# Linear attention and gated FFN in four layers: the second attention layer's queries of two token groups by seven block products

## The chip, the cores and the metric

The kernel runs on one core of one Trainium2 chip. The metric is the device time of one execution in microseconds (us); a lower time is better. The profiles are of one profiled execution each, with its own time beside its span (from the first to the last instruction).

## The reference

Four residual layers on a sequence of S = 2048 tokens with D = 1024: attention block A, FFN block B, A again, B again, with the same weights both times. Everything is bf16 at the boundary.

```python
def A_ref(x, wqkv, wo):             # H = 32 heads of 32
    q, k, v = split(x @ wqkv)
    phi = lambda t: where(t > 0, t + 1, exp(t)) + 1e-6
    pq, pk = phi(q), phi(k)
    kv = einsum("bhsd,bhse->bhde", pk, v)
    z = einsum("bhsd->bhd", pk)
    num = einsum("bhqd,bhde->bhqe", pq, kv)
    den = einsum("bhqd,bhd->bhq", pq, z)[..., None] + 1e-6
    return merge_heads(num / den) @ wo

def B_ref(x, w_gate, w_up, w_down): # F = 3584
    return ((x @ w_gate) * (x @ w_up)) @ w_down

x = x + A_ref(layernorm(x), wqkv, wo)
x = x + B_ref(layernorm(x), w_gate, w_up, w_down)
x = x + A_ref(layernorm(x), wqkv, wo)
x = x + B_ref(layernorm(x), w_gate, w_up, w_down)
```

## The kernel before

X (all 2048 x 1024 activations) stays in SBUF. Tokens are in 16 tiles of 128, four tiles to a group of 512, so there are four groups. SBUF work space is 17 `slots` of 8 KB a partition and 12 `temps` of 2 KB; PSUM is eight `banks` of 128 x 512 fp32. All three are queues: `get()` takes the one that was put back longest ago, at the time the program is written, so the order of the gets decides which physical bank an operation lands in and for whose last reader it waits. The order of instructions on each engine is the order in which the Python code issues them.

The layers are numbered `li` = 0 (attention), 1 (FFN), 2 (attention), 3 (FFN). `layer_A(li, ahead)` has two phases.

**Keys and values.** In layer 0 `kv_eight` makes them tile by tile with eight matmuls of 512 columns a block. In layer 2 `kv_seven` does it by a seven-product scheme (Strassen-Winograd): the weights and the transposed, normalized tokens are cut into 2 x 2 blocks, sums of blocks are made on VectorE (`w_sum`, `x_sum`), and a unit of 256 tokens of half a group needs seven products for K and seven for V, in the order `SEQ`, in place of eight each. ScalarE copies partial sums out of PSUM and VectorE adds them back. Five banks serve it (`bk`: ak, av, ck, cv, b), three more (`kvp`) gather K'V over all tokens in `kp` (line 533). The last two tiles' `kp` are left to `rest()`.

**Queries and outputs.** A loop over steps `i` runs one instruction sequence by steps of 128 features of a group (8 steps a group, 32 in all):

- `den_step` of step i - 4: one matmul for the denominators (line 801), Ln and Exp of it on ScalarE (803, 807), one multiply on VectorE (810);
- `q_step` of step i: eight matmuls of 512 columns (787), then phi: Exp on ScalarE (311), a minimum with add and a maximum with add on VectorE (312, 314);
- `fold` at steps 4 to 11, in which the K'V blocks are multiplied into `wo`, which was loaded by two DMAs of 1 MB on the SyncE (SP) queue, the first at plan step 90 of `kv_seven`, the second after its last unit;
- `out_step` of step i - 12: eight matmuls (818) and one add into X on VectorE (820).

At step 0 `rest()` and `finish_kv()` end the K'V sums and make the masked blocks `kvm`, `zb`. In layer 0 `scale_begin(1)` and `scale_end(1)` at steps 30 and 33 work out the scale of the down weights: a transpose on TensorE and some ten one-column steps on VectorE.

The last phase of the loop also carries what the next layer needs (`ahead`): LayerNorm of the first eight tiles (`ln_stats` 237 and 240, `ln_norm` 261 to 267, then a DMA transpose in `tr_tile`), the first two weight blocks (`W.load`; in the second FFN these come from a cache in DRAM), and block sums `t_sums`. Tile u has its three parts at steps 20 + 2u, 21 + 2u, 22 + 2u.

The FFN (`ffn_pass`, `quad`, `down_seven`) uses seven products as well: line 950 for gate and up, 1190 for down, both with 512 columns to a matmul. The one exception is the very last output block, two halves of which have 256 columns.

Of the kernel before, what the change touches and what calls it, by code (L numbers as in the profile page):

```python
# [9 lines left out]
ACT = mybir.ActivationFunctionType  # L10
# [25 lines left out]
def kernel(  # L36
# [11 lines left out]
    nc = tc.nc  # L48
# [37 lines left out]
    def v3(s, n):  # L86
        return s[:].rearrange("p (k n) -> p k n", n=n)
# [411 lines left out]
    def kv_seven(kvp):  # L499
        plan = {}  # L500

        def at(step, f, *args):
            plan.setdefault(step, []).append((f, args))
# [223 lines left out]
        return rest  # L727

    def layer_A(li, ahead):
        kvp = [banks.get() for _ in range(3)]  # L730
        rest = kv_eight(li, kvp) if li == 0 else kv_seven(kvp)

        kvx = slots.get()
        kvm, kvT, zb = (v3(kvx, P)[:, r * KD:(r + 1) * KD, :] for r in range(3))

        def finish_kv():
            for b in range(3):
                nb = min(3, KD - 3 * b)
                src = kvp[b][:, 0:nb * VW].rearrange("p (c f) -> p c f", f=VW)
                nc.vector.tensor_copy(out=z[:, 3 * b:3 * b + nb], in_=src[:, :, P])  # L740
                for j in range(nb):
                    if li == 0:
                        nc.vector.tensor_tensor(out=kvm[:, 3 * b + j, :], in0=src[:, j, 0:P], in1=mask[:],
                                                op=ALU.mult)
                    else:
                        nc.vector.scalar_tensor_tensor(out=kvm[:, 3 * b + j, :], in0=src[:, j, 0:P],
                                                       scalar=kaps[:, 2:3], in1=mask[:], op0=ALU.mult, op1=ALU.mult)
            for c in range(KD):
                nc.vector.tensor_scalar(out=zb[:, c, :], in0=mask[:], scalar1=z[:, c:c + 1], scalar2=None,
                                        op0=ALU.mult)  # L750
# [12 lines left out]
        def fold(c):  # L763
            if not M:
                M.extend(slots.get() for _ in range(DC))
            for n in range(DC):
                b = banks.get()
                nc.tensor.matmul(out=b[:], lhsT=kvT[:, c, :], rhs=v3(wA["o"][n], NB)[:, c, :], start=True, stop=True)  # L768
                if n == 0:
                    nc.scalar.copy(out=v3(M[n], NB)[:, c, :], in_=b[:])  # L770
                else:
                    nc.vector.tensor_copy(out=v3(M[n], NB)[:, c, :], in_=b[:])
                banks.put(b)
            if c == KD - 1:
                slots.put(*wA.pop("o"))

        pq = {}
        pqs = {}

        def q_step(g, c):  # L780
            w3 = h3 if li else v3
            xnT = w3(xnTs[(li, g)], NB)
            w = w3(wA["q"][c // (NB // P)], NB)
            j = c % (NB // P)
            b = banks.get()
            for k in range(KD):
                nc.tensor.matmul(out=b[:], lhsT=w[:, k, j * P:(j + 1) * P], rhs=xnT[:, k, :],  # L787
                                 start=(k == 0), stop=(k == KD - 1))
            pq[(g, c)] = temps.get()
            phi(b, pq[(g, c)][:].bitcast(BF16)[:, 0:G], 1 if li else None)  # L790
            banks.put(b)
            if c == KD - 1:
                slots.put(xnTs.pop((li, g)))
                if g == NG - 1:
                    slots.put(*wA.pop("q"))

        def den_step(g, c):
            t = pq.pop((g, c))
            p = t[:].bitcast(BF16)[:, 0:G]
            b = banks.get()  # L800
            nc.tensor.matmul(out=b[:], lhsT=zb[:, c, :], rhs=p, start=True, stop=True)  # L801
            r = temps.get()
            nc.scalar.activation(out=r[:], in_=b[:], func=ACT.Ln, bias=epss[:, 2:3] if li else eps6[:],
                                 scale=1.0)
            banks.put(b)
            rb = r[:].bitcast(BF16)[:, 0:G]
            nc.scalar.activation(out=rb, in_=r[:], func=ACT.Exp, scale=-1.0)
            if c == 0:
                pqs[g] = slots.get()
            nc.vector.tensor_tensor(out=v3(pqs[g], G)[:, c, :], in0=p, in1=rb, op=ALU.mult)  # L810
            temps.put(r, t)

        def out_step(g, j):
            tl, n = divmod(j, DC)
            t = g * TPG + tl
            b = banks.get()
            for c in range(KD):
                nc.tensor.matmul(out=b[:], lhsT=v3(pqs[g], G)[:, c, tl * P:(tl + 1) * P],  # L818
                                 rhs=v3(M[n], NB)[:, c, :], start=(c == 0), stop=(c == KD - 1))
            nc.vector.tensor_tensor(out=X[:, t, n * NB:(n + 1) * NB], in0=X[:, t, n * NB:(n + 1) * NB],  # L820
                                    in1=b[:], op=ALU.add)
# [7 lines left out]
        for i in range(NQ + OLAG):  # L829
            if i >= LAG and i - LAG < NQ:  # L830
                den_step(*divmod(i - LAG, KD))
            if i < NQ:
                q_step(*divmod(i, KD))
# [7 lines left out]
            if i >= OLAG:  # L841
                out_step(*divmod(i - OLAG, KD))
# [449 lines left out]
```

## Time and profile before

| | us |
|---|---|
| median of 3 runs | 1498.21 (1497.66 to 1498.67) |
| the profiled execution | 1497.95 |
| its span | 1496.0 |
| TensorE busy | 1489.4 (100% of the span) |
| VectorE busy | 986.6 (66%) |
| ScalarE busy | 811.0 (54%) |
| GpSimd busy | 89.9 (6%) |
| keys and values of the second attention layer | 758.24 to 865.4 |
| its queries and outputs | 865.4 to 985.05 |

In the profile PE is TensorE's matmuls, PEld its weight loads, DVE VectorE, ACT ScalarE, POOL GpSimd, SP SyncE. Rows of the timeline give start, duration, engine, line, operation, tiles, count; a merged row of several matmuls lasts from the first start to the modelled end of the last. Rows of the groups give count, then busy time and mean duration in ns, then the idle time before with what ended it. Rows of the chain of waits give start, duration and line of each piece of the chain that ended last.

### The profile page before, as it was taken

How to read it: one execution, taken by the hardware profiler on the slowest of the kernel's cores; microseconds unless marked ns; L12 is line 12 of the kernel's file. 1: busy time of each engine (PE TensorE's matmuls, PEld its weight loads, DVE VectorE, ACT ScalarE, POOL GpSimd, SP SyncE). 2: the span in 40 equal slices, each digit the busy share in tenths (PEclk: the TensorE clock that was granted, in tenths of full speed). 3: DMA queues.
4: the chain of work that ended last, by engine and by line, in shares of the span. 5: the costliest groups of instructions: out<-in, count | busy, mean ns of one | idle time of the engine just before them, and what ended most of it. 6: DMA issues, size and time to landing. Idle time of an engine off the chain costs nothing.

```text
span 1496.0 us, 18407 instructions
## 1 busy us (share of the span) xinstructions
PE 1489.4 (100%) x7121; PEld 685.0 (46%) x7121; DVE 986.6 (66%) x1662; ACT 811.0 (54%) x1184; POOL 89.9 (6%) x46
## 2 busy tenths in 40 slices
PE   9999999999999999999999999999999999999999
PEld 4454444444444444444444444444444444444444
DVE  6567989988677666657877686854445844444452
ACT  4678875777558477764557675623335213333420
POOL 0000004963000000000000000000000000000000
DMA  8696146465469788758531101464332788343613
GB/s 246 172 306 232 58 90 198 132 213 157 131 199 309 260 260 260 251 212 249 183 85 26 39 29 45 118 235 166 134 125 97 190 266 320 113 169 113 210 61 130
DMA packets 220087, 253.90 MB, mean 170 GB/s; under 512 B 68576, under 2 KB 196192, under 8 KB 209248
## 3 DMA queue, kind: packets, MB, share of 16 engines
q1 hardware_dynamic: 219712, 252.47, 53.5%
q8 instruction: 55, 0.90, 0.2%
q10 hardware_dynamic: 288, 0.26, 0.1%
q14 instruction: 32, 0.26, 0.1%
HBM read 196.08 MB, written 40.89 MB: 158 GB/s over the span
## 4 chain that ended last, share of the span: by engine, by line
PE 97%; DVE 2%; DMA 1%; ACT 0%; SPq 0%; issue 0%; DVEq 0%; ACTq 0%
PE b L950 45%; PE b L1190 23%; PE b L650 7%; PE b L787 7%; PE b L818 7%; PE b L579 6%; PE b L801 1%; DMA s<-in_A_wqkv_dram 1%; PE b L669 1%; PE b L768 0%; PE b L533 0%; DVE st L237 0%; ACT f L295 0%; DVE X L1163 0%; DVE X L820 0%; DVE s L301 0%
## 5 line engine op out<-in xcount | busy, mean ns | idle before, releaser
L950 PE MATMUL b<-s,s 128*128 128x512 f16 x3136 | 677.7, 379 | 0.0
L950 PEld LDWEIGHTS <-s 128*128 128x128 f16 x3136 | 306.8, 98 | 369.8
L1190 PE MATMUL b<-s,s 128*128 128x512 f16 (+1 forms) x1582 | 339.1, 377 | 0.0
L966 DVE TENSOR_TENSOR f<-f,b 128x512 f32<-128x512 f32 x232 | 159.1, 686 | 223.9 <-ACT f L955 209.7
L955 ACT COPY f<-b 128x512 f32<-128x512 f32 x284 | 166.2, 585 | 224.3 <-PE b L950 224.3
L1190 PEld LDWEIGHTS <-s 128*128 128x128 f16 x1582 | 154.8, 98 | 183.9
L961 ACT COPY b<-b 128x512 f32<-128x512 f32 x104 | 59.3, 570 | 128.3 <-PE b L950 128.3
L452 ACT ACTIVATE s<-s,scw 128x1024 f16<-128x1024 bf16 x112 | 122.8, 1151 | 1.9 <-DMA s<-in_B_w_gate_dram 1.8
L787 PE MATMUL b<-s,s 128*128 128x512 bf16 (+1 forms) x512 | 120.3, 379 | 0.0
L818 PE MATMUL b<-s,s 128*128 128x512 bf16 x512 | 118.5, 379 | 0.3 <-DVE s L810 0.3
L916 ACT ACTIVATE s<-s,scw 128x1792 f16<-128x1792 bf16 x48 | 83.0, 1784 | 62.4 <-DMA s<-in_B_w_down_dram 57.3
L650 PE MATMUL b<-s,s 128*128 128x512 bf16 x512 | 112.1, 379 | 1.2 <-DMA s<-in_A_wqkv_dram 0.5
L871 POOL TENSOR_SCALAR s<-s,scw 128x1024 f16<-128x1024 bf16 x28 | 88.3, 3170 | 258.2 <-DVE X L820 243.8
L970 DVE SCALAR_TENSOR_TENSOR s<-f,b 128x512 f16<-128x512 f32 x108 | 74.1, 686 | 40.1 <-PE b L950 24.6
L579 PE MATMUL b<-s,s 128*128 128x512 f16 x448 | 98.3, 379 | 0.2
L970 DVE SCALAR_TENSOR_TENSOR s<-f,f 128x512 f16<-128x512 f32 x116 | 83.3, 718 | 4.2 <-DMA dc<-s 0.3
L818 PEld LDWEIGHTS <-s 128*128 128x128 bf16 x512 | 50.0, 98 | 60.9 <-DVE s L810 0.9
L650 PEld LDWEIGHTS <-s 128*128 128x128 bf16 x512 | 49.7, 98 | 60.9 <-issue 1.4
L787 PEld LDWEIGHTS <-s 128*128 128x128 bf16 (+1 forms) x512 | 50.0, 98 | 59.4
L237 DVE BATCH_NORM_STATS2 st<-X 128x6 f32<-128x512 bf16 x112 | 71.6, 680 | 3.6 <-DMA X<-in_A_x_dram 3.6
L1098 DVE TENSOR_TENSOR s<-s,s 128x1024 f16<-128x1024 f16 x80 | 52.9, 677 | 23.4 <-PE b L1190 23.4
L579 PEld LDWEIGHTS <-s 128*128 128x128 f16 x448 | 43.6, 98 | 52.2 <-issue 1.2
(124 smaller groups left out, 1097.2 us busy)
## 6 DMA issues: line engine op xcount, KB each, us to landing
s<-wc SPq DMA_DIRECT2D x56, 1024.0 KB, 6.6
s<-dc SPq DMA_DIRECT2D x32, 896.0 KB, 5.6
wc<-s SPq DMA_DIRECT2D x28, 1024.0 KB, 5.2
s<-in_B_w_down_dram SPq DMA_DIRECT2D x24, 896.0 KB, 5.9
s<-in_A_wqkv_dram SPq DMA_DIRECT2D x17, 1024.0 KB, 8.0
s<-in_B_w_down_dram SPq DMA_DIRECT2D x14, 1024.0 KB, 8.0
s<-in_B_w_gate_dram SPq DMA_DIRECT2D x28, 512.0 KB, 6.6
s<-in_B_w_up_dram SPq DMA_DIRECT2D x28, 512.0 KB, 7.7
```

The lines of the kernel that those rows point to most:

```text
L452: nc.scalar.activation(out=h, in_=v, func=ACT.Copy, scale=scw[:, m:m + 1])
L579: nc.tensor.matmul(out=b[:], lhsT=lhs[i][:, k, pr * P:(pr + 1) * P], rhs=rhs[:, k, :], start=k == 0 and (i in (1, 5) or i == 2 and w == "v ...
L650: nc.tensor.matmul(out=b[:], lhsT=xnT[:, k, tl * P:(tl + 1) * P], rhs=w[:, k, :], start=(k == 0), stop=(k == KD - 1))
L787: nc.tensor.matmul(out=b[:], lhsT=w[:, k, j * P:(j + 1) * P], rhs=xnT[:, k, :], start=(k == 0), stop=(k == KD - 1))
L818: nc.tensor.matmul(out=b[:], lhsT=v3(pqs[g], G)[:, c, tl * P:(tl + 1) * P], rhs=v3(M[n], NB)[:, c, :], start=(c == 0), stop=(c == KD - 1))
L871: nc.gpsimd.tensor_scalar(out=h3(s, D)[:, i, :], in0=v3(s, D)[:, i, :], scalar1=scw[:, 2:3], scalar2=None, op0=ALU.mult)
L916: nc.scalar.activation(out=v.bitcast(F16)[:, r * w:(r + 1) * w], in_=v[:, r * w:(r + 1) * w], func=ACT.Copy, scale=scw[:, 2:3])
L950: nc.tensor.matmul(out=o[m][:], lhsT=W.get(j, m, st[i - 1], k), rhs=mv[i - 1][:, k, :], start=start and k == 0, stop=stop and k == KH - 1, ...
L955: nc.scalar.copy(out=d[m][:], in_=o[m][:])
L966: nc.vector.tensor_tensor(out=d[m][:], in0=d[m][:], in1=o[m][:], op=ALU.add)
L970: nc.vector.scalar_tensor_tensor(out=h3(hs[h], 2 * G)[:, pos, g * G:(g + 1) * G], in0=x[:], scalar=HS, in1=y[:], op0=ALU.mult, op1=ALU.mult)
L1190: nc.tensor.matmul(out=bank[(key, tl)][:, cols], lhsT=lhs(i, j, tl), rhs=h3(wd[2 * pi + j // WPC], NB)[:, j % WPC, cols], start=(j == 0 an ...
```

## The change

In layer 2 the queries of groups 2 and 3 (steps 16 to 31) are no longer made by `q_step` but by `q_part`: four units of four steps, each unit half of the features of one group. A unit makes seven products out of blocks of `wq` (`w_sum("q", 0..3)` at steps 12, 13, 14, 16) and the token sums that `kv_seven` made for the group and that are kept now. Each product is two times four matmuls of 256 columns into the two halves of a bank. Four banks are taken for it (two `a`, `b`, `c`), one slot for fp32 sums (`w`) and one for phi (`p`), both double-buffered. Steps k = 0 to 3 of a unit:

- k = 0: product 1 into a, copy a to b (ScalarE), product 5 into c, then the end of the denominator, then phi of the wide half of the unit before (1024 columns, `q_wide`);
- k = 1: product 6 into a, copy into w;
- k = 2: product 7 into a, copy into w, add of c, product 2 into b, phi of b;
- k = 3: product 4 into a, phi of a, product 3 into c, add of c. In the last unit the wide phi is done here, in two halves.

In `den_step` the matmul is issued first, and Ln, Exp and multiply follow in `end()`, behind the copies of the unit. Denominators of the units lag six steps in place of four; outputs pause at steps 22, 26, 30 and end three steps later. In both attention layers `rest()` and `finish_kv()` move from step 0 to step 1, `scale_end(1)` from 33 to 36. In layer 2 the norms for the next layer go by a list of steps, each part two steps after the statistics and the transposes a step later, and `W.load` goes from 22 and 28 to 24 and 32. In `kv_seven` the five banks are drawn ahead of the three of K'V and in another order, and `wo` is loaded in four halves after the last unit.

```diff
@@ kv_seven
-        at(90, lambda: wA.update(o=[load_cols(wo_v, 0)]))
-
-        bk = {key: banks.get() for key in ("ak", "av", "ck", "cv", "b")}
+        bk = {key: banks.get() for key in ("ak", "b", "ck", "av", "cv")}
+        kvp.extend(banks.get() for _ in range(3))
...
-            if u % 2 == 1:
+            if u in (1, 3):
                 slots.put(xgs.pop(u // 2))
...
-        wA["o"].append(load_cols(wo_v, 1))
+        wA["o"] = [slots.get() for _ in range(DC)]
+        for r in range(0, KD, KH):
+            for n in range(DC):
+                nc.sync.dma_start(out=v3(wA["o"][n], NB)[:, r:r + KH, :],
+                                  in_=wo_v[:, r:r + KH, n * NB:(n + 1) * NB])
@@ layer_A
-        kvp = [banks.get() for _ in range(3)]
+        kvp = [banks.get() for _ in range(3)] if li == 0 else []
...
+        def q_wide(un, hs=(0, 2)):
...
+            x = wd2[:, hs[0] * NB:hs[1] * NB]
+            m, e = phi_exp(x, 1)
+            return lambda: phi_end(w4(x), pv[:, 2 * hs[0]:2 * hs[1], 2 * P:G], 1, m, w4(e))
+
+        def q_part(un, k, den):
...
+            def prod(o, i, start):
+                w = w_rhs("q", i)
+                for e in range(2):
+                    for kk in range(KH):
+                        nc.tensor.matmul(out=o[:, e * 2 * P:(e + 1) * 2 * P], lhsT=w[:, kk, (2 * r + e) * P:(2 * r + e + 1) * P],
+                                         rhs=mvq[i][:, kk, :], start=start and e == 0 and kk == 0, stop=kk == KH - 1,
+                                         skip_group_check=True)
...
+            if k == 0:
+                prod(a, 1, True)
+                nc.scalar.copy(out=b[:], in_=a[:])
+                prod(c, 5, True)
+                den()
+                if un > 0:
+                    q_wide(un - 1)()
+            elif k == 1:
+                prod(a, 6, False)
+                nc.scalar.copy(out=wd2[:, 0:NB], in_=a[:])
+                den()
+            elif k == 2:
+                prod(a, 7, False)
+                nc.scalar.copy(out=wd2[:, NB:D], in_=a[:])
+                add(1)
+                den()
+                prod(b, 2, False)
+                narrow(b, 0)()
+            else:
+                prod(a, 4, False)
+                if last:
+                    q_wide(un, (1, 2))()
+                end = narrow(a, 1)
+                prod(c, 3, False)
+                add(0)
+                den()
+                if last:
+                    end_w = q_wide(un, (0, 1))
+                end()
...
         def den_step(g, c):
...
             nc.tensor.matmul(out=b[:], lhsT=zb[:, c, :], rhs=p, start=True, stop=True)
-            r = temps.get()
-            nc.scalar.activation(out=r[:], in_=b[:], func=ACT.Ln, ...)
...
+            def end():
+                r = temps.get()
+                nc.scalar.activation(out=r[:], in_=b[:], func=ACT.Ln, ...)
...
+            return end
...
-        LAG, OLAG = 4, 12
...
+        Q8 = 2 * KD if li else NQ
+        NQU = (NQ - Q8) // 4
+        dens = {i + (4 if i < Q8 else 6): i for i in range(NQ)}
+        outs = [i for i in range(12, NQ + (15 if Q8 < NQ else 12)) if Q8 == NQ or i not in (22, 26, 30)]
...
+            if Q8 <= i < NQ:
+                q_part(*divmod(i - Q8, 4), den)
+            else:
+                den()
+                if i < Q8:
+                    q_step(*divmod(i, KD))
+            if Q8 < NQ and i in (12, 13, 14, 16):
+                w_sum("q", min(i - 12, 3))
-            if i == 0:
+            if i == 1:
                 rest()
                 finish_kv()
...
-            if li == 0 and i == 33:
+            if li == 0 and i == 36:
                 scale_end(1)
@@ ahead_of
-            at(20 + 2 * u, ln_stats, li, u)
-            at(21 + 2 * u, ln_norm, li, u)
-            at(22 + 2 * u, tr_tile, li, u)
-        at(22, W.load, 0)
-        at(28, W.load, 1)
+            s, n = (20 + 2 * u, 1) if li == 1 else ((15, 17, 19, 20, 23, 27, 33, 35)[u], 2)
+            at(s, ln_stats, li, u)
+            at(s + n, ln_norm, li, u)
+            at(s + n + 1, tr_tile, li, u)
+        at(22 if li == 1 else 24, W.load, 0)
+        at(28 if li == 1 else 32, W.load, 1)
```

More of the change, by code (lines that the diff above doesn't have):

```diff
@@ L795, in q_step, with w4 @@
                     slots.put(*wA.pop("q"))
-        def den_step(g, c):
-            t = pq.pop((g, c))
-            p = t[:].bitcast(BF16)[:, 0:G]
+        qu = {}
+        def q_wide(un, hs=(0, 2)):
+            wd2 = qu["w"][:].bitcast(F32).rearrange("p (u n) -> p u n", n=D)[:, un % 2]
+            pv = qu["p"][:].rearrange("p (u c n) -> p u c n", u=2, n=G)[:, un % 2]
+            def w4(x):
+                return x.rearrange("p (c n) -> p c n", n=2 * P)
+            x = wd2[:, hs[0] * NB:hs[1] * NB]
+            m, e = phi_exp(x, 1)
+            return lambda: phi_end(w4(x), pv[:, 2 * hs[0]:2 * hs[1], 2 * P:G], 1, m, w4(e))
@@ new lines, in q_part, with w2, narrow, add @@
+        def q_part(un, k, den):
+            g, r = 2 + un // 2, un % 2
+            if not qu:
+                qu.update(a=[banks.get(), banks.get()], b=banks.get(), c=banks.get(), w=slots.get(), p=slots.get())
+            a, b, c = qu["a"][un % 2], qu["b"], qu["c"]
+            wd2 = qu["w"][:].bitcast(F32).rearrange("p (u n) -> p u n", n=D)[:, un % 2]
+            pv = qu["p"][:].rearrange("p (u c n) -> p u c n", u=2, n=G)[:, un % 2]
+            b11, b21, b12, b22, t = x_blocks(g)
+            mvq = {1: b11, 2: b21, 3: b22, 4: t[:, 3], 5: t[:, 0], 6: t[:, 1], 7: t[:, 2]}
+            def prod(o, i, start):
[5 more added lines that the diff above has]
+                                         skip_group_check=True)
+            def w2(x):
+                return x.rearrange("p (c n) -> p c n", n=2 * P)
+            last = un == NQU - 1
+            def narrow(o, j):
+                m, e = phi_exp(o[:], 1)
+                return lambda: phi_end(w2(o[:]), pv[:, 2 * j:2 * j + 2, 0:2 * P], 1, m, w2(e))
+            def add(n):
+                v = wd2[:, n * NB:(n + 1) * NB]
+                nc.vector.tensor_tensor(out=v, in0=v, in1=c[:], op=ALU.add)
+            if k == 0:
[27 more added lines that the diff above has]
+                end()
+                if last:
+                    end_w()
+                    slots.put(qu["w"])
+                if r == 1:
+                    slots.put(xnTs.pop((li, g)), xgs.pop(g))
+                if last:
+                    slots.put(*wA.pop("q"), wS.pop("q"), wS.pop("d"))
+                    banks.put(*qu.pop("a"), qu.pop("b"), qu.pop("c"))
@@ L800, in den_step @@
+        def den_step(g, c):
+            if (g, c) in pq:
+                t = pq.pop((g, c))
+                p = t[:].bitcast(BF16)[:, 0:G]
+            else:
+                un, j = 2 * (g - 2) + c // 4, c % 4
+                j = (j + 2) % 4 if un == NQU - 1 else j
+                c, t = 2 * (c // 4) + j % 2 + 4 * (j // 2), None
+                p = qu["p"][:].rearrange("p (u c n) -> p u c n", u=2, n=G)[:, un % 2, j]
             b = banks.get()
             nc.tensor.matmul(out=b[:], lhsT=zb[:, c, :], rhs=p, start=True, stop=True)
-            r = temps.get()
@@ L803, in den_step @@
[L803 to L811, printed above, removed]
+            def end():
+                r = temps.get()
+                nc.scalar.activation(out=r[:], in_=b[:], func=ACT.Ln, bias=epss[:, 2:3] if li else eps6[:],
+                                     scale=1.0)
+                banks.put(b)
+                rb = r[:].bitcast(BF16)[:, 0:G]
+                nc.scalar.activation(out=rb, in_=r[:], func=ACT.Exp, scale=-1.0)
+                if c == 0:
+                    pqs[g] = slots.get()
+                nc.vector.tensor_tensor(out=v3(pqs[g], G)[:, c, :], in0=p, in1=rb, op=ALU.mult)
+                temps.put(r)
+                if t:
+                    temps.put(t)
+                elif (un, j) == (NQU - 1, 1):
+                    slots.put(qu["p"])
@@ L824, in out_step @@
                 slots.put(pqs.pop(g))
-        LAG, OLAG = 4, 12
         rows = {}
         NQ = NG * KD
[L829 to L833, printed above, removed]
-            if i == 0:
+        Q8 = 2 * KD if li else NQ
+        NQU = (NQ - Q8) // 4
+        dens = {i + (4 if i < Q8 else 6): i for i in range(NQ)}
+        outs = [i for i in range(12, NQ + (15 if Q8 < NQ else 12)) if Q8 == NQ or i not in (22, 26, 30)]
+        outs = {i: n for n, i in enumerate(outs)}
+        for i in range(max(outs) + 1):
+            den = den_step(*divmod(dens[i], KD)) if i in dens else lambda: None
+            if Q8 <= i < NQ:
+                q_part(*divmod(i - Q8, 4), den)
+            else:
+                den()
[4 more added lines that the diff above has]
+            if i == 1:
                 rest()
@@ L840, in layer_A @@
                 fold(i - 4)
-            if i >= OLAG:
-                out_step(*divmod(i - OLAG, KD))
+            if i in outs:
+                out_step(*divmod(outs[i], KD))
             if li == 0 and i == 13:
```

## The prediction

> **What bounds the kernel now.** I read the page's head first, then the chain of waits, then the stages of the second attention layer, then TensorE's rows in order of time.
>
> ```profile
> span 1496.0 us, 18407 instructions
> PE 1489.4 (100%) x7121; PEld 685.0 (46%) x7121; DVE 986.6 (66%) x1662; ACT 811.0 (54%) x1184; POOL 89.9 (6%) x46
> ...
> PE 97%; DVE 2%; DMA 1%; ACT 0%; SPq 0%; issue 0%; DVEq 0%; ACTq 0%
> ```
>
> TensorE (PE) works the whole span and holds 97% of the chain that ends last. Time can fall only if PE gets fewer columns to stream or loses one of its few waits; it rises if another engine makes PE wait. The stage in question, as a window (PE, weight loads, DVE, ACT, POOL busy; granted clock; DMA), and its rows:
>
> ```profile
> 865.40:985.05 119.65, 119.65 (x565) 54.53 (x563) 93.35 (x190) 72.33 (x120) 0.00 (x0) 1.00 0.27 83
> ...
> 890.29 1.89 PE L787 MATMUL b<-s,s 128*128 128x512 f16 x8
> 892.02 1.89 PE L818 MATMUL b<-s,s 128*128 128x512 bf16 x8
> 893.75 0.38 PE L801 MATMUL b<-f,s 128*128 128x512 bf16 x1
> ...
> 1491.19 1.69 PE L1190 MATMUL b<-s,s 128*128 128x256 f16 x14
> ```
>
> PE never waits here, at clock 1.00. Eight matmuls of 512 columns go from 890.29 to 892.02: 1.73 us, 0.216 each; the row's 1.89 holds a tail of 0.16 that overlaps the next. A step of query (1.73), denominator (0.22) and output (1.73) is 3.68 us. Fourteen 256-column matmuls with a new weight each take 1.69 − 0.16 = 1.53 us: 0.109 each, half of 0.216.
>
> **The products (the term that counts).** Groups 2 and 3 lose 16 query steps of 8 matmuls: 128 × 0.216 = 27.7 us. They get 4 units of 7 products of 8 half-width matmuls: 224 × 0.109 = 24.4 us. Gain 3.2 us, if PE keeps running. The same number of denominators and outputs stays.
>
> **The waits that go.** Three chains, from the chain of waits and the timeline:
>
> ```profile
> 757.79 2.73 DVE X L1163 x4
> 760.60 0.58 ACT b L584
> 761.22 5.35 PE b L579 x24
> ...
> 758.24 25.08 PE L579 MATMUL b<-s,s 128*128 128x512 f16 x112
> ...
> 864.34 0.61 DVE vb L566
> 864.99 0.63 PE b L533 x8
> ...
> 864.00 0.64 PE L533 MATMUL b<-vb,s 128*128 128x129 bf16 x8
> ...
> 233.45 0.21 DVE wq L402
> 234.70 0.03 DVE kap L419
> 237.78 0.25 DVE s L810
> 238.09 2.12 PE b L818 x9
> ...
> 234.39 3.40 PE L818 MATMUL b<-s,s 128*128 128x512 bf16 x15
> ```
>
> *Bank order.* K/V of the second attention layer starts at 758.24 while DVE still empties the last four down-projection banks (757.79, four reads). Four of its five banks are among those; 6k, the fourth product, starts at 761.22 where 758.24 + 12 × 0.216 = 760.83 was due: 0.39 us lost. Now its five banks are drawn first and the late ones go to K'V, whose first matmul comes a unit later. Gain 0.39; what is late next, the copy into bank b, follows product 1k and has two products (1.7 us) of cover.
>
> *Last K/V sums.* Eight K'V matmuls start at 864.00, the next eight at 864.99; at 0.059 each (0.63 − 0.16 over 8) they were due at 864.47: 0.52 us waiting for `vb`. A query step later `vb` is there. Gain 0.52. In exchange `finish_kv` moves behind the phi of query 1:
>
> ```profile
> 868.40 1.38 DVE L749 TENSOR_SCALAR s<-mask,z 128x128 bf16<-128x128 bf16 x8
> ...
> 871.09 0.38 PE L801 MATMUL b<-f,s 128*128 128x512 bf16 x1
> ```
>
> The first denominator needs the first of the eight `zb` pieces. They start about 1.77 us later (a query step), so the first is ready near 870.4, and the denominator is due 0.52 earlier, at 870.57. I take nothing, with 0 to 0.3 loss as bounds. In the first layer nothing waits there before, and the room is as wide; zero.
>
> *scale_end(1) from step 33 to 36.* In the first layer output 24 (fifteen matmuls from 234.39) should go on at 237.63 and does at 238.09: 0.46 us, for the last L810. DVE's chain before it holds the scale's small steps from 233.45 to 234.83. Without that 1.4 us the multiply is ready in time: gain 0.46 (0 if ScalarE were the later one). The small steps run later, under eight outputs; POOL's casts, which need the scale, start after that.
>
> **What the units cost the other engines.** Durations by group, of this stage and of the K/V stage, which has the same forms (the last is the 2048-wide sum; the weight load is for a rival):
>
> ```profile
> L311 ACT ACTIVATE f<-b,lns,kaps 128x512 bf16<-128x512 f32 x31 | 24.0, 773 | 11.5 <-PE b L787 10.5 <-DVE f L314 1.0
> L314 DVE SCALAR_TENSOR_TENSOR f<-b,f 128x512 bf16<-128x512 f32 x32 | 22.1, 692 | 1.1
> L803 ACT ACTIVATE f<-b,epss 128x512 f32<-128x512 f32 x32 | 22.1, 691 | 20.9 <-PE b L801 20.9
> L820 DVE TENSOR_TENSOR X<-X,b 128x512 bf16<-128x512 bf16 x31 | 21.0, 678 | 3.0 <-PE b L818 3.0
> L807 ACT ACTIVATE f<-f 128x512 bf16<-128x512 f32 x32 | 20.1, 630 | 1.0
> L810 DVE TENSOR_TENSOR s<-f,f 128x512 bf16<-128x512 bf16 x32 | 13.2, 412 | 8.9 <-ACT f L807 8.8
> L312 DVE TENSOR_SCALAR f<-f,scw,epss 128x512 bf16<-128x512 bf16 x31 | 12.8, 412 | 13.0 <-ACT f L311 13.0
> L237 DVE BATCH_NORM_STATS2 st<-X 128x6 f32<-128x512 bf16 x16 | 10.2, 680 | 0.0
> L267 DVE TENSOR_SCALAR xn<-X,mv,rstd 128x1024 f16<-128x1024 bf16 x8 | 4.3, 541 | 0.0
> L787 PEld LDWEIGHTS <-s 128*128 128x128 f16 x246 | 24.1, 98 | 28.9
> ...
> L571 DVE TENSOR_TENSOR s<-s,b 128x512 f32<-128x512 f32 x16 | 10.9, 680 | 0.6 <-ACT s L589 0.6
> L301 DVE SCALAR_TENSOR_TENSOR s<-s,f 128x1024 bf16<-128x1024 f32 x8 | 9.8, 1225 | 0.3
> L299 DVE TENSOR_SCALAR f<-f,scw,epss 128x1024 bf16<-128x1024 bf16 x8 | 4.4, 546 | 9.3 <-ACT f L295 9.3
> L295 ACT ACTIVATE f<-s,lns,kaps 128x1024 bf16<-128x1024 f32 x8 | 9.9, 1240 | 8.1 <-DVE s L571 8.1
> L589 ACT COPY s<-b 128x512 f32<-128x512 f32 x16 | 9.4, 586 | 4.8 <-PE b L579 4.8
> ...
> L204 DVE TENSOR_TENSOR s<-s,s 128x2048 f16<-128x2048 f16 x3 | 3.6, 1198 | 0.0
> ```
>
> A middle unit (four steps, three outputs): PE 56 × 0.109 + 4 × 0.22 + 3 × 1.73 = 12.2 us. ACT: three copies 1.76, two narrow exponentials 1.55, a wide one 1.24, four Ln and Exp pairs 5.28: 9.8 us. DVE: two adds 1.36, two narrow phi ends 2.21, a wide one 1.77, four multiplies 1.65, three output adds 2.03: 9.0, and a tile's norm (two statistics 1.36, one scaling 0.54) makes 10.9. Both fit, DVE at 90%. Unit 1 (steps 20 to 23) is the tight one: two tiles' norms and only two denominators, DVE 12.0 us against PE's 7 × 0.87 + 2 × 0.22 + 3 × 1.73 = 11.7. Unit 0 has 12.9 against 13.9, with `w_sum` 3; the first three sums (1.2 us each) go beside steps 12 to 14, where DVE's 2.2 of 3.68 us become 3.4. Rows' durations overlap their successors by some 0.07, so DVE is at PE's speed in unit 1, not beyond.
>
> I lay the steps out from the start of step 16, each engine in its order. PE can wait at three places a unit. Copy of product 7 ahead of product 4: in PE order a denominator, product 2 and a denominator lie between (1.3 us), the reader starts 0.2 after the product and takes 0.59; room 0.3. Add of product 5 ahead of product 3: DVE comes from unit 1's norms at about 23.3 us, PE wants it at 23.0: 0.3 lost. Denominator of the wide halves at step k = 2: from the unit's start ACT needs product 1, copy, pair and wide Exp (4.6 us), then DVE 0.55 and 1.23: 6.3 against PE's 6.5; where DVE still runs statistics it is late, by 0.1 in unit 2. So PE loses some 0.4; bounds 0 and 1.5 (0.3 to 0.4 at each of four places, since the rooms are that small). Four banks remain for denominators and outputs; one is wanted again two steps later, and the adds that free it lag by up to 3 us against 4.7 or more. No wait.
>
> **Loads and the tail.**
>
> ```profile
> s<-in_A_wo_dram SPq DMA_DIRECT2D x4, 1024.0 KB, 8.6
> ...
> s<-xn SPq DMA_TRANSPOSE x60, 3.1
> ```
>
> `wo` comes in four halves, on SP; the second waits for 3k of the last unit, near 860. The first two halves, 1 MB, land within 8.6 us, by 869, and the fold starts near 872; the others have four folds more. Nothing else is queued on SP before step 18. The FFN's second block load moves from step 28 to 32 and holds SP until the last wide phi is read; the transposes behind it are issued at steps 36 and 38 anyway. The last lands 3.1 us later, so the block sum on DVE at step 39 waits for it and the output adds queue behind; all eight banks are free again by then, seven outputs of 1.73 us cover it. Zero. If that cover went, some 2 us.
>
> **Sum.** −3.2 − 0.39 − 0.52 − 0.46 + 0.4 = −4.2 us. The profiled execution takes 1497.95 us (span 1496.0 and 1.95 around it): 1493.75. It lies 0.26 under the median of the runs, 1498.21, so 1494.0 for the median. About 0.2%, 3 us, is what a measurement of this kernel can tell from no change.
>
> **Rivals.** *First, small waits in every unit.* ACT and DVE are in order and their rooms are 0.2 to 0.3 us. If a wide phi meets a pair of statistics (1.36) each time it is due, PE loses about 1 us in three units: +3 instead of +0.4, 1496.6, no difference that can be told. For: DVE at 90 to 100%. Against: in units 2 and 3 the norms come a step away from the wide phi. Chance 0.19.
>
> *Second, slower: VectorE sets the pace.* The phi ends now write 2 × 256 and 4 × 256 pieces of a tile; no row shows that form. If a scattered result costs nothing, it is 0.69 and 1.23; if it doubles those ends, a unit gets 2 × 0.69 + 1.23 = 2.6 us more, DVE 13.5 in a middle unit and 14.6 in unit 1, 1.3 to 2.9 over PE, and one bank after another comes late: with a unit 0 of 14.3 (+0.4) some +6 in all, and half as much again where DVE's lag delays the ACT steps that wait for it: 1493.6 without waits and +9, 1502.6. It takes the whole gain from 1.15 us of excess a unit (4.6 over four) and ends slower by 3 us from 1.9. Against: the K/V stage's adds write `vb` in four pieces (L566) at the ordinary time. Chance 0.13.
>
> *Third, half-width matmuls do not halve.* If the weight load (0.098) lay bare beside each: 224 × 0.207 = 46.4, +18.7 against the old steps, 1515. The row of 14 speaks against it, at 0.109 with a load each. Chance 0.02. The Trainium skill ("TensorE: Matmul & The Clock Gate", section Back-to-back issue gap) gives a sustained spacing for pairs of weight load and matmul of about 81 ns at 128 columns and 131 at 512; by it, as an estimate on a line between, 256 columns take 98, and the units cost 22.0 against 16.8 us: 5 us slower. The trace disagrees at every width (59 ns at 129, 109 at 256, 216 at 512), so the measurements decide.
>
> **How the numbers follow.** My forecast has 0.66; its own range, waits of 0 to 1.5, is 1493.6 to 1495.1. Adding the first rival's up to 1497.5 leaves under 0.2 out; the low end takes 0.6 more for the spread of runs: 1493.0. Faster by over 0.2%: 0.66 and a little of the first rival, 0.67; within: 0.18; slower: the second and third, 0.15.
>
> **What would show it.** Right: 224 matmuls of 128x256 in L827 with 109 ns from start to start; no chain through L1163, L584 at the start of K/V, none through L566 at K'V, none through L402 to L810 in the first layer's tail; PE idle of some tenths in steps 22 to 30, before L892 or L827, for DVE. Wrong: idle at every unit, then which of the three places tells the first rival; L301 of 128x2x256 over 0.8 us the second; spacing over 120 ns the third.

## The result and the profile after

The changed kernel takes 1493.62 us, median of 7 runs (1492.38 to 1494.24); the kernel before took 1497.9 beside it (7 runs, 1497.1 to 1499.49). The ratio is 0.997, 95% interval 0.9958 to 0.9981: faster by 4.3 us. The profiled execution of after takes 1493.62 us with a span of 1491.8.

The head of its page, and the share by engine of the chain that ended last:

```profile
span 1491.8 us, 18614 instructions
PE 1485.7 (100%) x7217; PEld 694.1 (47%) x7217; DVE 995.3 (67%) x1668; ACT 813.7 (55%) x1193; POOL 89.8 (6%) x46
...
PE 96%; DMA 2%; DVE 1%; ACT 0%; SPq 0%; issue 0%
```

TensorE lost 3.7 us of busy time and still holds the chain. VectorE got 8.7 us more to do. DMA's share of the chain rose from 1% to 2%.

The stage of the second attention layer's queries and outputs as one window, and units 0 to 3 within it as another (columns: length, then busy time of PE, weight loads, DVE, ACT, POOL; granted clock; DMA share, GB/s), and three groups of the stage:

```profile
861.71:980.80 119.09, 119.09 (x684) 65.56 (x682) 103.62 (x199) 76.92 (x132) 0.00 (x0) 1.00 0.32 99
903.69:954.00 50.31, 50.31 (x345) 33.65 (x344) 43.51 (x82) 35.58 (x64) 0.00 (x0) 1.00 0.28 74
```

```profile
L827 PE MATMUL b<-s,s 128*128 128x256 f16 x224 | 27.1, 273 | 0.0
...
L301 DVE SCALAR_TENSOR_TENSOR s<-b,f 128x512 bf16<-128x512 f32 x8 | 5.5, 692 | 0.5
...
L301 DVE SCALAR_TENSOR_TENSOR s<-s,f 128x1024 bf16<-128x1024 f32 x4 | 4.9, 1226 | 0.1
```

The 224 half-width matmuls are there (273 ns is one row with its modelled tail, which the next one overlaps), and PE is busy for the whole stage: no wait in any unit. DVE is at 86% in the units. The phi ends, whose results now go to two or four separate pieces of a tile, take 692 and 1226 ns, against 692 and 1225 for whole results before.

Where the 4.2 us of span came from, measured between the first matmuls of the stages in both traces:

| stage | before, us | after, us | difference |
|---|---|---|---|
| start, up to the first query of layer 0 | 126.57 | 126.20 | -0.37 |
| first attention, queries and outputs | 123.83 | 123.37 | -0.46 |
| first FFN | 507.84 | 508.49 | +0.65 |
| second attention, keys and values | 104.04 | 103.65 | -0.39 |
| second attention, queries and outputs | 122.77 | 119.09 | -3.68 |
| second FFN | 507.83 | 507.83 | 0.00 |

Three waits are gone. The PE rows at the last K/V sums (timeline), then the chain of waits at the end of the first attention layer, then the chain at the start of K/V:

```profile
861.71 3.62 PE L790 MATMUL b<-s,s 128*128 128x512 f16 x16
865.16 1.11 PE L532 MATMUL b<-vb,s 128*128 128x129 bf16 x16
866.11 1.24 PE L790 MATMUL b<-s,s 128*128 128x512 f16 x5
```

```profile
233.92 0.22 PE b L892
234.13 3.45 PE b L916 x16
237.59 0.06 PE b L400
237.64 2.37 PE b L916 x11
```

```profile
758.23 7.78 PE b L578 x36
...
769.19 0.60 DVE vb L565
769.79 0.61 DVE s L570
770.39 0.02 issue
770.42 1.24 ACT f L295
771.66 0.48 ACT vb L612
772.14 0.04 issue
772.18 3.88 PE b L578 x17
```

The sixteen K'V matmuls (L532) run through from 865.16 to 866.11, 0.059 each. The outputs of the first layer go on at 237.64 after the small matmul of the scale (L400). K/V runs without a break from its first matmul at 758.07 to a wait near 772. That wait, 0.30 us before 772.18 and 0.05 after it, was there before the change too: the ScalarE copy of product 4 of V (L612) stands behind the exponential of 1024 columns (L295, 1.24 us).

One wait is new, in the first FFN. A load of cached down weights, issued at 466.26, lands 7.56 us later. The first fence is the chain of waits there, the second the window of that stretch, with the columns of the windows above:

```profile
465.69 0.52 SPq L101
466.21 0.05 issue
466.26 7.56 DMA s<-dc
473.82 0.04 issue
473.86 6.20 PE b L1297 x28
```

```profile
466.00:473.80 7.80, 7.33 (x34) 3.22 (x33) 5.60 (x10) 4.20 (x7) 0.00 (x0) 1.00 0.98 287
```

PE stood for 0.70 us before 473.86 (start to start, less one matmul). In the profile of the kernel before it waits 0.02 us there. This load accounts for the +0.65 of the table. So the -4.2 us is made up of -3.16 (products: the -3.68 of the table less the 0.52 of the last K/V sums), -1.37 (three waits), +0.70 (this load) and -0.37 (the start). The start is scatter: in the thirteen profiles the first query of layer 0 comes between 125.04 and 126.72 us, whatever the kernel.

### The profile page after: what moved, and what is told of

Same layout as the page of the kernel before. It is cut to its first block, busy times and chain, and to the rows that moved or that the text cites. A ratio compares the mean times of both kernels' runs of the same rounds, so it can differ in the third digit from the quotient of the medians.

```text
span 1491.8 us, 18614 instructions
## 1 busy us (share of the span) xinstructions
PE 1485.7 (100%) x7217; PEld 694.1 (47%) x7217; DVE 995.3 (67%) x1668; ACT 813.7 (55%) x1193; POOL 89.8 (6%) x46
## 4 chain that ended last, share of the span: by engine, by line
PE 96%; DMA 2%; DVE 1%; ACT 0%; SPq 0%; issue 0%
PE b L1057 45%; PE b L1297 21%; PE b L916 7%; PE b L653 7%; PE b L578 6%; PE b L790 6%; PE b L827 2%; DMA s<-in_A_wqkv_dram 1%; PE b L892 1%; DMA s<-dc 1%; PE b L532 1%; PE b L672 1%; PE b L771 0%; DVE s L1205 0%; DVE f L1270 0%; ACT s L338 0%
## 5 line engine op out<-in xcount | busy, mean ns | idle before, releaser
L790 PE MATMUL b<-s,s 128*128 128x512 bf16 (+1 forms) x384 | 90.1, 379 | 0.0
L237 DVE BATCH_NORM_STATS2 st<-X 128x6 f32<-128x512 bf16 x112 | 71.6, 680 | 3.3 <-DMA X<-in_A_x_dram 3.3
L1270 DVE SCALAR_TENSOR_TENSOR X<-b,kap,f 128x512 bf16<-128x512 f32 x48 | 32.7, 744 | 39.2 <-PE b L1297 39.2
```

## The experiments

Experiments that ran together share a chip and the runs of the kernel before: e1 to e4 with 1497.77 us (24 runs), e5 to e8 with 1498.05 (11 runs), e9 to e11 with 1498.14 (10 runs). Waits of PE are given start to start, less the matmul's own spacing; the view of waits counts from the modelled end and shows some 0.2 us less or nothing.

### e1 and e2: the waits without the products, the products without the waits

e1 is the kernel before with the bank order, the last K/V sums a step later and `scale_end` at 36:

```diff
-        bk = {key: banks.get() for key in ("ak", "av", "ck", "cv", "b")}
+        bk = {key: banks.get() for key in ("ak", "b", "ck", "av", "cv")}
+        kvp.extend(banks.get() for _ in range(3))
...
-        kvp = [banks.get() for _ in range(3)]
+        kvp = [banks.get() for _ in range(3)] if li == 0 else []
...
-            if i == 0:
+            if i == 1:
...
-            if li == 0 and i == 33:
+            if li == 0 and i == 36:
```

e2 is after with these same lines put back.

> The kernel before with three edits alone: bank order in kv_seven, the last K/V sums at step 1, scale_end(1) at step 36. All queries by eight products. If the three waits go and nothing comes back: TensorE's waits of 0.39 (near 761), 0.52 (864) and 0.46 us (238) are gone and the span is 1.4 us shorter than before. If the first layer's 0.46 is given back at the cached down-weight load near 473 (where after waits 0.70 us): those three gone, a new wait of 0.4 to 0.7 there, and a span 0.9 us shorter.

> The changed kernel with the three edits of waits undone (old bank order, last K/V sums at step 0, scale_end(1) at step 33); the units, the order of copies and the norms stay. My sum: 224 half-width matmuls in place of 128 full ones, 3.2 us less than before, the three old waits in their places, none near 473. If the units had cost waits of 0.4 us that the three edits hide: 2.8 us less, with idle time of TensorE between 904 and 955.

e1: 1496.06 us (11 runs), ratio 0.9989 (0.998 to 0.9997). Of its PE waits after the start only 0.36 is left (the one near 772, here at 770.34), where before has 1.73 in all: 1.37 less. The span of its profile is 3.0 us shorter than before's, because its start was 1.5 us shorter as well.

e2: 1494.31 us (8 runs), ratio 0.9977 (0.9967 to 0.9987). The three waits are back (0.46 near 237, 0.15 and 0.25 near 760, 0.52 at 864), none is in the units. Its last matmul ends 3.72 us earlier than before's, 0.53 of it at the start: 3.19 for the products. Its view of PE's waits (engine and line that waited, what for, us in total, times, longest) shows the one at the last K/V sums and the one in the first layer:

```profile
PE b L531 <- DVE vb L564: 0.4, 1, 0.4
...
PE b L915 <- DVE s L902: 0.3, 1, 0.3
```

The two parts add up: 3.19 + 1.37 = 4.56, and after shows 3.16 + 1.37 beside the load wait and the start.

### e3 and e11: the scale's step back to 33, all else as after

```diff
-            if li == 0 and i == 36:
+            if li == 0 and i == 33:
```

> The changed kernel with scale_end(1) back at step 33. If what the first layer gains is given back at the down-weight load: a wait of 0.46 us returns near 238, the one near 473 shrinks from 0.70 to about 0.25, and the end of the first FFN and the span stay within 0.2 us. If the load's wait is independent: it stays at 0.7 and the span grows by 0.46 us.

> scale_end(1) at step 33 once more. If the first layer's gain is given back at the load only when TensorE comes early: the 0.46 us near 238 again and a wait near 473 that is 0.46 us smaller than where step 36 comes equally early (0 to 0.25). If the two have nothing to do with each other: waits near 473 of the same sizes as with step 36.

e3 took 1493.59 us (one run) with a span of 1491.8, as after's: the wait near 238 is back (0.455) and the one near 473 is gone, so nothing was won or lost against that execution of after. That pointed to the earlier finish of layer 0 being given back at the load. e11, the same kernel once more, took 1493.68 (one run): 0.458 near 238 and also 0.114 near 473. So the load wait does not need the step at 36. From the first query of layer 0 to the last matmul, which leaves the start out, e3 and e11 take 1361.95 and 1362.07 us; with the step at 36, e10 below takes 1361.58 and the profile of after, with its long wait for the load, 1362.16.

### e10: after once more

> The changed kernel once more, for the wait near 473 that one execution showed (0.70 us) and the prediction did not have. If it hangs on when the load happens to land: another size, 0 to 0.7 us, all else the same. If it is fixed in the kernel's order: 0.7 us again.

1493.07 us (6 runs), ratio 0.9967 (0.9955 to 0.9979). In its profile the wait near 473 is 0.12. Over all profiles with the scale at 36 it was 0.70, 0.30, 0.27, 0.21, 0.12, 0.11 and 0 (e1); with 33 it was 0, 0, 0 and 0.11. So it is not a fixed wait of this order of steps, and DMA is at 98% in that stretch of after, as it is in the kernel before (0.98, 287 GB/s as well).

The traces show why it varies. Counted from the first matmul of the down projection, PE wants this load at 54.39 us (e1, e2 and e3, which do not wait). In ten profiles, all but those of after, e8 and e9, it landed at 54.18 to 54.65, the kernel before with 54.37 among them: there was no room before the change either. In the profile of after it landed at 55.04, and the delay did not arise in the load itself, which took 7.56 us (7.27 to 7.63 in the ten). ScalarE had stood 4.68 us, up to 447.07, for a scanning load (weights of the attention whose squares it sums, `scan_a`), against 3.99 to 4.33 us in the other twelve profiles. What follows on ScalarE, VectorE and SP up to the issue of the late load came later too: it was issued at 47.48 on this count, against 46.78 to 47.18 in the ten. Why the scanning load was late in that execution stays open, and whether a finish 0.46 us earlier makes the wait longer the few executions do not settle.

### e4: the norms at their old steps

```diff
-            s, n = (20 + 2 * u, 1) if li == 1 else ((15, 17, 19, 20, 23, 27, 33, 35)[u], 2)
+            s, n = 20 + 2 * u, 1
```

> The changed kernel with the norms for the second FFN at their old steps (statistics 20 + 2u, scaling 21 + 2u, transposes 22 + 2u), so that units 1 to 3 each carry two tiles: VectorE 12.8 us by my rows against TensorE's 11.7 to 12.2. Theory (VectorE at TensorE's speed, small rooms): waits of 0.6 to 1.2 us a unit, 1.5 to 3 us more than after. Rival (rooms are larger than I laid out, the spread of the norms is not needed): no wait, the time of after.

1497.29 us (11 runs), ratio 0.9999 (0.999 to 1.0008): the whole gain is gone. PE waits 1.6 us in the units and 2.1 us at the outputs of the last group, more than the 1.5 to 3 us of the theory, which had them in the units alone. Two lines of the view of PE's waits, and two rows of the timeline (in brackets: idle time before, and what ended it):

```profile
PE b L916 <- DVE s L903: 1.8, 2, 0.9
...
PE b L827 <- DVE s L842: 0.6, 2, 0.4
```

```profile
966.51 0.29 ACT L261 ACTIVATE rstd<-mv,eps5x 128x1 f32<-128x1 f32 x1 [1.29 <-DVE mv L240]
...
968.79 0.39 PE L916 MATMUL b<-s,s 128*128 128x512 bf16 x1 [0.95 <-DVE s L903]
```

ScalarE stood 1.29 us at `rstd` of a norm (the reciprocal standard deviation, one column), which wants the statistics (L240) that VectorE had just begun, and the Ln and Exp of the next denominator (L896, L900) were queued behind it. In e4 ScalarE waits in this way at seven of the eight `rstd`, 0.79 to 2.15 us each time; in after it waits at none, since the statistics are done 0.1 to 4.3 us before. So the list of norm steps is what keeps the first rival away; products alone would have met it. e4 changes two things at once, the distance between a norm's parts and the number of tiles that fall into the units, and no run separates them.

### e5: denominators ahead of the copies

```diff
             if k == 0:
+                den()
                 prod(a, 1, True)
                 nc.scalar.copy(out=b[:], in_=a[:])
                 prod(c, 5, True)
-                den()
...
                 prod(a, 6, False)
-                nc.scalar.copy(out=wd2[:, 0:NB], in_=a[:])
                 den()
+                nc.scalar.copy(out=wd2[:, 0:NB], in_=a[:])
```

and in the same way at k = 2 and k = 3.

> The changed kernel with the ends of the denominators (Ln, Exp, multiply) issued ahead of the units' copies and adds in each step, so that ScalarE copies product 7 only after a pair of 1.32 us. By my rows the copy then starts 0.46 us later against a room of 0.3 before product 4: 0.2 us of wait in each of three units, some 0.6 us in all. Rival (the room is larger than laid out): no wait, the time of after.

1493.6 us (5 runs), ratio 0.9968 (0.9956 to 0.998): no difference from after by time. In the trace PE waits three times, 0.11 each, ahead of product 4, less than the 0.6 expected. PE's timeline at one of the three:

```profile
936.91 0.38 PE L892 MATMUL b<-s,s 128*128 128x512 bf16 x1
937.24 1.47 PE L827 MATMUL b<-s,s 128*128 128x256 f16 x12
```

Product 4 was due 0.22 after the denominator, at 937.13. In unit 1 the copy of product 7 starts 1.46 us after the product does, against 1.07 in after (0.39 later, expected 0.46). In after it ends at 925.50, 0.31 ahead of product 4, as large a room as the prediction's 0.3. So the copies' place ahead of the denominators is worth 0.34 us in all, no more.

### e6 and e7: more work for VectorE in every wide phi

After each wide phi end the same values are written once more (e6) or twice more (e7). That is 1.23 us each time for the wide halves of units 0 to 2, which fall into units 1 to 3; those of the last unit, written in two halves of 0.69 us in its last step, get it too:

```diff
-            return lambda: phi_end(w4(x), pv[:, 2 * hs[0]:2 * hs[1], 2 * P:G], 1, m, w4(e))
+            d = pv[:, 2 * hs[0]:2 * hs[1], 2 * P:G]
+
+            def fin():
+                phi_end(w4(x), d, 1, m, w4(e))
+                for _ in range(1):
+                    nc.vector.scalar_tensor_tensor(out=d, in0=w4(x), scalar=0.0, in1=w4(e), op0=ALU.max, op1=ALU.add)
+            return fin
```

> The changed kernel with VectorE's last step of each wide phi done twice (same values): 1.23 us more a unit, unit 1 at 13.2 us by my rows against TensorE's 11.7. Theory (VectorE at TensorE's speed): waits of 2 to 3 us in the units. Rival (durations overlap by enough that a unit has over 1.2 us of room): under 0.5 us.

> The same with that step done three times, 2.45 us more a unit, about the excess of my second rival (2.6 us if scattered results took twice as long). By that rival's working: waits of 6 to 9 us, the span at about the one of before plus 2 to 4. If VectorE's backlog is caught up in units 2 and 3: 3 to 5 us.

e6: 1496.7 us (one run), 3.1 over e5, which ran beside it. PE waits 2.94 us in the units: 0.53 and 0.59 in unit 1, 0.91 in unit 2, 0.91 in unit 3, as the theory had it. A row of its PE timeline, at the start of unit 2's third step (k = 2), where PE wants the denominator of a wide half:

```profile
937.94 0.39 PE L898 MATMUL b<-s,s 128*128 128x512 bf16 x1 [0.75 <-DVE s L816]
```

Of 1.23 us added, 0.91 came out as waiting, 1.12 in unit 1. So VectorE had 0.3 us left in units 2 and 3 and 0.1 in unit 1. The extra work in the last step brought no wait.

e7: 1501.74 us (one run), 8.1 over e5. PE waits 6.7 us, within the 6 to 9 of the rival's working: 1.79 and 0.59, then 2.17, then 2.17. The view of PE's waits, and a row of windows from the last of these on (granted clock in the third column from the end):

```profile
PE b L898 <- DVE s L816: 5.6, 3, 2.0
```

```profile
954.40:955.50 1.10, 1.09 (x9) 0.90 (x10) 1.10 (x3) 0.00 (x0) 0.00 (x0) 0.99 0.07 15
955.50:958.80 3.30, 3.30 (x17) 2.20 (x15) 2.37 (x5) 3.00 (x5) 0.00 (x0) 0.50 0.41 77
958.80:970.00 11.20, 11.20 (x59) 5.59 (x58) 10.93 (x20) 8.02 (x13) 0.00 (x0) 1.00 0.22 73
```

The wait ends at 954.41, and from 955.5 to 958.9 PE runs at half clock: fourteen matmuls of 256 columns take about 0.213 in place of 0.109 and one of 512 takes 0.427 in place of 0.216, another 1.7 us. 6.7 + 1.7 = 8.4 for 7.4 us of added work (three units by two times 1.23; the work added in the last step again brought no wait).

### e8 and e9: a version with the waits left in after taken out

e8 moved one tile's statistics out of the chain that ends at 772 and the sum over the next down weights two plan steps on:

```diff
-            at(i, ln_stats, 2, t, (0,))
+            at(i + 2 if i == 8 else i, ln_stats, 2, t, (0,))
...
-                        at(2 + 9 * i, scan_a, i, -1)
+                        at(2 + 9 * i + 2 * (i == 5), scan_a, i, -1)
```

> The changed kernel with two moves for the waits that are left: in kv_seven the statistics of plan step 8 two steps later, out of the chain that holds ScalarE's copy of product 4 in the first unit (0.35 us near 772); in the first FFN's down projection the last of the scanning loads (step 47) two steps later, behind the cached down-weight load that TensorE waited for near 473 (0.70 us in the one execution of after). If both chains are what I read: both waits gone, 0.35 us less than after in every run and up to 1 us where the load was late. If another chain takes their place (the next reader of that bank, another load): a wait of like size close behind.

1493.62 us (6 runs), ratio 0.9968 (0.9956 to 0.998): no gain, a miss. The chain of e8 at K/V:

```profile
769.22 0.61 DVE f L237
769.83 0.02 issue
769.85 0.21 DVE mv L240
770.06 0.56 DVE s L570
```

The statistics (L237, L240) landed inside the same chain, between L565 and L570, and the wait at 772 grew from 0.35 to 0.77. At 473 nothing waited, but 0.20 at 479.67: ScalarE's cast of weights stood behind its squares of the scanning load, which now landed later (its first square starts at 474.04, after 6.45 us of waiting).

e9 moves the statistics behind that chain (plan step 12, the scaling and transpose with them), the late load to plan step 49 and its sums to 65 and 72:

```diff
-            at(i, ln_stats, 2, t, (0,))
+            at(12 if i == 8 else i, ln_stats, 2, t, (0,))
...
-                at(i + 5, ln_norm, 2, t)
-                at(i + 6, tr_tile, 2, t)
+                at(i + (7 if i == 8 else 5), ln_norm, 2, t)
+                at(i + (8 if i == 8 else 6), tr_tile, 2, t)
...
-                        at(2 + 9 * i, scan_a, i, -1)
-                        at(10 + 9 * i, scan_a, i, 0)
-                        at(13 + 9 * i, scan_a, i, 1)
+                        at(2 + 9 * i if i < 5 else 49, scan_a, i, -1)
+                        at(10 + 9 * i if i < 5 else 65, scan_a, i, 0)
+                        at(13 + 9 * i if i < 5 else 72, scan_a, i, 1)
```

> The changed kernel with the two moves of the first try mended: the statistics of plan step 8 go to step 12 (behind the add that the wide exponential waits for) with their norm at 15; the last scanning load stays behind the cached down-weight load, and ScalarE reads it at steps 65 and 72, behind the casts of the next weight pieces. If the chains are now read rightly: no wait near 772, 473 and 479, 0.35 to 1 us less than after. If the first product of the second unit waits for something else near 772: 0.3 us stays.

1492.82 us (5 runs, 1491.99 to 1493.01), ratio 0.9964 (0.9952 to 0.9977), span 1490.2. The chains at 765 and at 466:

```profile
764.94 11.22 PE b L578 x52
```

```profile
465.84 16.19 PE b L1297 x75
```

Both are one unbroken piece of PE, and PE waits nowhere after the start. It is clearly under the kernel before; it is 0.25 us under after beside it (1493.07, e10), where the waits of the profiles say 0.12 + 0.35 = 0.47, and both are too little for these runs to tell.

## Why the prediction was right

It gave 1494.0 us (1493.0 to 1497.5), by 1493.75 for the profiled execution, which measured 1493.62. By its steps:

- **Products, -3.2:** right, 3.16 in after and 3.19 in e2. Half-width matmuls with a new weight each go at 0.109, so the third rival (weight loads laid bare) is out, and so is the sum by the spacing that the Trainium skill gives ("TensorE: Matmul & The Clock Gate", section Back-to-back issue gap), which made the units a loss.
- **Three waits, -0.39, -0.52, -0.46:** right, each seen in its stage (the first in two pieces, 0.15 and 0.25) and together as 1.37 in e1. Nothing came late in their place: the first denominator did not wait for `zb` (the stage has no PE idle), and the copy into bank b had its cover.
- **Waits in the units, +0.4:** the term that was mis-sized; measured 0. The step that failed is the add of product 5 in unit 1, which I had VectorE finish 0.3 us after PE wanted it. VectorE's and PE's rows there:

```profile
924.80 0.63 DVE L918 TENSOR_TENSOR X<-X,b 128x512 bf16<-128x512 bf16 x1
925.36 0.54 DVE L267 TENSOR_SCALAR xn<-X,mv,rstd 128x1024 f16<-128x1024 bf16 x1
925.81 0.68 DVE L842 TENSOR_TENSOR s<-s,b 128x512 f32<-128x512 f32 x1
...
925.81 1.91 PE L827 MATMUL b<-s,s 128*128 128x256 f16 x16
```

Products 4 and 3 are the sixteen matmuls from 925.81; product 3 begins with the ninth, at 926.68. The add ends at 926.49: 0.19 to spare in place of 0.3 too late. PE's side of the layout was right: product 3 begins 23.0 us after the start of step 16, as laid out. VectorE's add ends 22.8 us after it, not 23.3. Each row of VectorE starts before the one ahead of it has ended (0.56 after its start for 0.63, 0.45 for 0.54). From the start of unit 1 to the end of this add VectorE runs sixteen instructions whose durations sum to 9.72 us, and they take 8.94. The prediction named this overlap, 0.07 a row; a layout by full durations comes out too late by the amount that was missed and more, but the prediction does not show the layout itself, so that this is the reason is an inference. The other 0.1 us, for the denominator of the wide half in unit 2, was not there either: the wide phi ends at 935.39, and PE takes up that denominator at 935.79.
- **Rival 1 (waits in every unit):** not so here. Waits in the units do come in e4, with the old norm steps, but 2.1 of the 3.7 us that PE waits there fall at the outputs of the last group, a place that the rival did not name. **Rival 2 (VectorE sets the pace):** its premise fell, since a scattered result costs nothing in these two forms (692 and 1226 ns). Its price came near in part by luck: it named 2.6 us a unit and +9, of which some +6 for the waits and half as much again for ScalarE held up behind VectorE; e7 put in 2.45 and lost 8.1, 6.7 of it in waits, and 1.7 to the half clock that the rival did not have. e6 puts the point from which VectorE decides at 0.1 to 0.3 us a unit for the first wait, so "at PE's speed in unit 1, not beyond" held.
- **Loads and the tail, 0:** right for the second attention layer; its block sum did wait for the last transpose (0.55 us before 970.14) and PE did not notice. What the prediction lacked is the load near 473 us in the first FFN, which had no room in the kernel before either: +0.70 in this execution and 0 to 0.30 in others. It also could not know the start's -0.37. These two give +0.33 and the missing +0.4 of the units takes away as much, so that the total fits to 0.13 us is in part luck.

## What to carry to other kernels

When an engine runs without a break, a change to it is priced by its own instructions (here 128 × 0.216 against 224 × 0.109), and the risk lies in how little room its neighbours have left; adding one known piece of work to a neighbour, as e6 does for VectorE, measures that room (0.1 to 0.3 us here). What stands in an in-order queue behind a wait counts as much as the work itself: the same norms cost nothing when spread out with their parts two steps apart, and the whole gain at their old steps, one step apart. An advantage of a few tenths can be eaten or faked by a load that lands a little earlier or later, so look at the stage it came from, in several executions, before putting it down to an edit.

## What the runs showed of the hardware

The half clock of e7 came after a wait of 2.17 us; the same wait 14 us before it, and one of 1.79 before that, did not bring it. It set in 1.1 us after PE was running again and lasted 3.41 us. The Trainium skill ("TensorE: Matmul & The Clock Gate", section Part 1, The HAM clock gate) has the clock fall to half after at least one idle window of about 3.4 us; the length of the slow stretch agrees with that window, but the idle time before it was shorter, and half clock began when PE was busy.

The trace suggests why only the third wait brought it. In e7 the granted clock first goes up at 6.57 us, down at 955.48, up at 958.89 and down again after the last matmul at 1501.61: 278, 279 and 438 steps of 3.4133 us after the first change. So the clock changes here only at the edges of a fixed grid, and in the other ten profiles that show changes of the clock the last one lies on such a grid too (435 or 436 steps after the first). The third wait (952.24 to 954.41) lies whole between the two edges 952.06 and 955.48, which makes that step of the grid 64% idle. The second (937.90 to 940.07) is cut by the edge at 938.41 into 0.51 and 1.66 us, the first (923.37 to 925.16) by the one at 924.76 into 1.39 and 0.40, so no step there was more than 49% idle. A decision at each edge, by how idle the step before it was, fits all three; with one slow stretch in one run it is an inference, and no run tests it.

It may not be confined to e7: three of e4's eleven runs, its slowest (1498.45 to 1498.62 us), show a mean granted clock of 0.999, as e7 does, and the profiled run of e4, its fastest, shows 1.000. No trace of those three is at hand, so this is not shown.
